# A spectral layer and an ELU block on one core: the second projection's weights and its stationary tiles at other SBUF addresses

## The chip, the cores and the metric

The kernel runs on one core of a Trainium2 chip. The metric is device time in microseconds (us). The profiled execution took 911.36 us; three timed runs have a median of 912.44 us (912.34 to 914.53).

## The reference, cut to what matters

`x` is 8 batches of 3008 tokens by 256 channels. A spectral layer comes first, then a two-layer block with an ELU:

```python
X = np.fft.rfft(x, axis=1)                       # per batch, along the tokens
Yr = Xr @ w_r - Xi @ w_i + b_r                   # complex 256 x 256 product
Yi = Xr @ w_i + Xi @ w_r + b_i
Y  = shrink(Yr) + 1j * shrink(Yi)                # toward zero by 0.01
y  = np.fft.irfft(Y, n=3008, axis=1)             # back to 24064 x 256 in all
h  = y @ w_in                                    # 256 -> 2048
g  = np.where(h > 0, h, np.exp(np.minimum(h, 0)) - 1)
out = g @ w_out                                  # 2048 -> 256
```

## The kernel before, in words

**The two halves.** The Fourier transforms are done as small matrix products with tables that the kernel builds for itself at the start. They are cut into units, named A, X, M, B and Y, whose matmuls stand at L144, L175, L192, L244 and L282. Between units the data goes to device memory and comes back in another layout (stores `DA<-A`, `DB<-Bz`, loads `Z<-DA`, `Bs<-DB`). The first batch's units run alone. Those of each later batch are laid out by `plan` between the steps of the block on the batch before, one unit per step or none.

**A step of the block.** The loop at the end of the kernel makes 376 steps: 47 blocks of 512 tokens times 8 *pairs* `fp` of hidden tiles (a tile is 128 of the 2048 hidden features, so a pair is 256). Step `i` does this:

- `front` (L705) fills a PSUM tile `hps` with four matmuls in bf16 of 512 columns (L715; a few are cut in two at a batch's end) and ScalarE takes the exponential into `Et` (L724, L726, L727 or L729).
- `finish_elu` (L734) has VectorE write the ELU of the step before into an SBUF tile `gT` (L740 or L742), 1024 elements of float32 per partition, and with that frees the step's `hps`. Two `hps` buffers take turns, and a third is used in some steps.
- `back` (L757) runs for the step two earlier (`LAG = 2`). Its eight matmuls (L773) have a 128 by 128 piece of `gT` as their stationary operand and one of the sixteen 1 KB pieces of `w_out_r` as their moving operand of 256 columns, both in the 4-byte type float32r. They add into two PSUM tiles `ps_o`, which after eight pairs are copied out (L784) and stored.

All engines' instructions run in the order in which they are written; the Tile layer adds the waits.

**The tiles of the change.** `w_out_r` is one tile of 16 pieces of 1 KB per partition, back to back. It is loaded in two halves by POOL's DMA queue (`load_w_out`, L583): the first half before the first batch's X units, the second (needed from `fp` = 4) after a small `gate` copy on POOL that waits for a load of `Bs`. `gT` comes from a pool of three buffers of 4096 bytes. The same three buffers hold, once, near the start, two tiles `A` of the second batch (L133): ScalarE and VectorE fill them and the SP queue stores them to `DA` (L157), from where `Z` of that batch is loaded (L164).

In the built kernel, `w_out_r` starts at byte 41,792 of every partition and the three `gT` buffers at 210,048, 214,144 and 218,240. The two `A` tiles take the first and the third of these. The pool gives the steps 0 and 1 the second buffer, both of them, step 2 the first and step 3 the third; from there on the three take turns.

Of the kernel before, what the change touches and what calls it, by code (L numbers as in the profile page):

```python
# [10 lines left out]
BF16 = mybir.dt.bfloat16  # L11
F32 = mybir.dt.float32
F32R = mybir.dt.float32r
# [16 lines left out]
def kernel(  # L30
# [11 lines left out]
    nc = tc.nc  # L42
    P = nc.NUM_PARTITIONS

    B, S, D = x.shape
    assert D == 256 and S == N1 * N2
    DFF = moe_w_in.shape[1]
    E = moe_w_out.shape[1]
    assert E == 256 and DFF % (2 * P) == 0
    NFT = DFF // P  # L50
# [5 lines left out]
    constp = ctx.enter_context(tc.tile_pool(name="constp", bufs=1))  # L56
# [4 lines left out]
    wcat_r = constp.tile([P, 2, 2 * D], BF16, name="wcat_r")  # L61
    wcat_s = constp.tile([P, 2, 2 * D], BF16, name="wcat_s")
    w_in_s = constp.tile([P, 2, DFF], BF16, name="w_in_s")
    w_out_r = constp.tile([P, NFT, E], F32R, name="w_out_r")
    bias_bc = constp.tile([P, 2 * D], F32, name="bias_bc")
    bias_p = constp.tile([P, 2 * D], BF16, name="bias_p")
    lam_n = constp.tile([P, 1], F32, name="lam_n")
# [22 lines left out]
    TB = 512  # L90
# [4 lines left out]
    n = B * PER  # L95
# [3 lines left out]
    A_of = {}  # L99
# [18 lines left out]
    def unit_ps(name, alone):  # L118
        if alone:
            return pre2.tile([P, 2, 512], F32, name=name, tag="pre2")  # L120
        return psF.tile([P, 2, 512], F32, name=name, tag="fps")

    def evac(dst, src, on_dve):
        if on_dve:
            nc.vector.tensor_copy(dst, src)  # L125
        else:
            nc.scalar.copy(dst, src)  # L127

    def unit_A(b, u, alone=False, on_dve=False, ahead=False):
        ci, uu = u // 2, u % 2  # L130
        if uu == 0:
            if ahead and ci > 0:
                A_of[b, ci] = late3.tile([P, 8, D], BF16, name="A", tag="gT")  # L133
            elif alone:
                A_of[b, ci] = wk4.tile([P, 8, D], BF16, name="A", tag="Bs")
            else:
                A_of[b, ci] = wk2.tile([P, 8, D], BF16, name="A", tag="A")
            if ci == 0:
                DA_of[b] = dram.tile([NJ, P, D], BF16, name="DA", tag="DA")
        xt, A = xts[ci], A_of[b, ci]  # L140
        dav = DA_of[b].rearrange("j p d -> p j d")
        ps = unit_ps("aps", alone or ahead)
        for j in range(2):
            nc.tensor.matmul(  # L144
                ps[:, j, :], lhsT=M1[:],
                rhs=xt[:, 4 * uu + 2 * j : 4 * uu + 2 * j + 2, :], start=True, stop=True,
            )
        evac(
            A[:, 4 * uu : 4 * uu + 4, :].rearrange("p n d -> p (n d)"),
            ps[:].rearrange("p a b -> p (a b)"), on_dve,  # L150
        )
        j0 = 8 * ci
        if alone:
            j0 += 4 * uu
            nc.sync.dma_start(dav[:, j0 : j0 + 4, :], A[:, 4 * uu : 4 * uu + 4, :])
        elif uu == 1:
            nc.sync.dma_start(dav[:, j0 : j0 + 8, :], A[:])  # L157
# [155 lines left out]
    with tc.tile_pool(name="stagep", bufs=1) as stagep:  # L313
# [186 lines left out]
        def fA(u):  # L500
            unit_A(0, u, alone=True)
            if u < 5:
                idle_pe(3)
# [60 lines left out]
    gatep = ctx.enter_context(tc.tile_pool(name="gatep", bufs=2))  # L564
    late2 = ctx.enter_context(tc.tile_pool(name="late2", bufs=2))
    late3 = ctx.enter_context(tc.tile_pool(name="late3", bufs=3))

    w_in_v = moe_w_in.rearrange("(c p) f -> p c f", p=P)
    w_out_v = moe_w_out.rearrange("(t p) e -> p t e", p=P).bitcast(F32R)
# [10 lines left out]

    def load_w_out(hh):
        hf = slice(hh * NFT // 2, (hh + 1) * NFT // 2)
        nc.gpsimd.dma_start(w_out_r[:, hf, :], w_out_v[:, hf, :])  # L583

    def gate(src):

# [9 lines left out]
    for ci in range(3):  # L596
        load_x(1, ci)
    load_w_out(0)
    nc.vector.tensor_scalar(w3[:], v3[:], CMAGIC, -CMAGIC, ALU.add, ALU.add)
    nc.vector.tensor_tensor(w3[:], v3[:], w3[:], ALU.subtract)  # L600
# [62 lines left out]
    for u in range(6):  # L663
        unit_A(1, u, on_dve=bool(u % 2), ahead=True)
        if u == 1:
            scale_w_in(1, True)
            for w in (2, 3):
                load_Bs(0, w)
            gate(Bs_of[0, 2][:, 0, 0:1])
            load_w_out(1)  # L670
            load_w_in(3)
        idle_pe(2)
# [22 lines left out]
    def pieces(t, k):  # L695

        out_, c = [], 0
        while c < k:
            b, r = divmod(t + c, S)
            e = min(k, c + S - r)  # L700
            out_.append((b, r, c, e))
            c = e
        return out_
# [29 lines left out]

    def finish_elu():  # L734
        for i, hps, Et, whole, halves in late_elu:
            gT = late3.tile([P, 2, TB], F32R, name="gT", tag="gT")
            for s in range(2) if halves else (slice(0, 2),):
                o, h, e = gT[:, s], hps[:, s], Et[:, s]
                if whole:
                    nc.vector.scalar_tensor_tensor(o, e, -1.0, h, ALU.add, ALU.max)  # L740
                else:
                    nc.vector.scalar_tensor_tensor(o, h, 0.0, e, ALU.max, ALU.add)  # L742
            g_of[i] = gT
        late_elu.clear()
# [12 lines left out]
    def back(i, split):  # L757
        blk, fp = divmod(i, NPAIR)
        bs = blk * TB
        gT = g_of.pop(i)  # L760
        nq = TB // P // 2
        if fp == 0:
            po_of[blk] = [
                psO.tile([P, 2, E], F32, name="ps_o", tag="outp") for _ in range(nq)
            ]
        po = po_of[blk]
        order = [(q, s) for q in range(nq) for s in range(2)]
        if i == n - 1:
            order = [(q, s) for s in range(2) for q in range(nq)]
        for q, s in order:  # L770
            ft = 2 * fp + s
            for i_ in range(2 * q, 2 * q + 2):
                nc.tensor.matmul(  # L773
                    po[q][:, i_ % 2, :], lhsT=gT[:, s, i_ * P : i_ * P + P],
                    rhs=w_out_r[:, ft, :], start=(ft == 0 and i_ % 2 == 0),
                    stop=(ft == NFT - 1), skip_group_check=True,
                )
        if fp < NPAIR - 1:
            return
        osb = late2.tile([P, 4, E], F32, name="osb", tag="osb")  # L780
        last = i == n - 1
        for q in range(nq):
            copy = nc.vector.tensor_copy if (last and q) or (split and q == 0) else nc.scalar.copy
            copy(osb[:, 2 * q : 2 * q + 2, :], po[q][:])  # L784
            for i_ in range(2 * q, 2 * q + 2):
                for b, t, c0, c1 in pieces(bs + i_ * P, P):
                    ov = out[b * S : b * S + S, :].rearrange("(r w j) e -> w r j e", w=4, j=8)
                    while c0 < c1:
                        w, r0 = t // WT, t % WT // 8
                        k = min(c1 - c0, (w + 1) * WT - t)  # L790
                        (nc.scalar if last and i_ % 2 == 0 else nc.sync).dma_start(
                            ov[w, r0 : r0 + k // 8], osb[c0 : c0 + k, i_, :]
                        )
                        t, c0 = t + k, c0 + k
        del po_of[blk]

    def put(kind, b, *a):
        return ({"A": unit_A, "X": unit_X, "M": unit_M, "B": unit_B, "Y": unit_Y}[kind], (b, *a))
# [45 lines left out]
    for i in range(n + LAG):  # L844
        if i < n:
            r = i % PER
            if r == 0:
                f0, f1 = plan(i // PER)
                used = [bool(u0 or u1) for u0, u1 in zip(f0, f1)]
            free = not used[r]  # L850
            bare = bare + 1 if free else 0
            calm = free and (i >= n - 2 or (r + 2 < PER and not used[r + 1] and not used[r + 2]))
            for f, a in f0[r]:
                f(*a)
            on_act = any(f is unit_M for f, a in f0[r])
            h = front(i, calm and bare % 3 == 1, on_act, free and i > 0)
        finish_elu()
        if i < n:
            for f, a in f1[r]:
                f(*a)  # L860
            split = i > LAG and (i - LAG) % NPAIR == NPAIR - 1
            if split:
                back(i - LAG, True)
            elu(i, *h, free and i > 0, on_act)
        else:
            split = False
        if i >= LAG and not split:
            back(i - LAG, False)
# [30 lines left out]
```

## Time and profile before

| what | us |
|---|---|
| profiled execution | 911.36 |
| its span, from first to last instruction | 909.6 |
| median of three timed runs | 912.44 |
| PE (TensorE matmuls) busy | 893.2, 98% of the span |
| VectorE busy | 717.5, 79% |
| ScalarE busy | 696.8, 77% |
| POOL busy | 314.9, 35% |
| granted TensorE clock, mean | 0.997 |

The profile has one row for each group of equal instructions: line, engine, operation, the tile written and those read, shapes, count, then the time in which at least one of them ran, the mean duration of one in ns, and the idle time in front of them with what ended it. PE is the row of the matmuls, PEld that of the loads of stationary operands (LDWEIGHTS), which run beside matmuls. Since matmuls overlap, the mean duration of one is longer than the time from one start to the next; where this document speaks of the *spacing*, it is the time between the starts of two neighbours, read from the single records of the trace.

### The profile page before, as it was taken

What the parts mean: (1) busy time and instruction counts of PE and PEld (TensorE: products, weight loads), DVE (VectorE), ACT (ScalarE), POOL (GpSimd) and SP (SyncE); (2) the same over time, 40 slices, a digit from 0 to 9 for tenths busy, and PEclk for the clock granted to TensorE, in tenths of its full rate; (3) what the DMA queues carried; (4) which work ended last, traced back from release to release, by engine and by line L of the source; (5) the groups of instructions that cost most, each with busy time, mean ns of one, the idle gap of its engine ahead of it and who ended that gap; (6) DMA issues with size and microseconds to landing.
All of it is one profiled execution on the core that took longest, in us unless ns stands there. A gap on an engine that the chain in (4) does not pass through costs nothing.

```text
span 909.6 us, 17270 instructions
## 1 busy us (share of the span) xinstructions
PE 893.2 (98%) x6721; PEld 652.3 (72%) x6721; DVE 717.5 (79%) x891; ACT 696.8 (77%) x850; POOL 314.9 (35%) x438
## 2 busy tenths in 40 slices
PE   8989999999999999999999999999999999999997
PEld 3447667876688667886678766787667866777775
DVE  8669778887788778897788877888778877778776
ACT  6768788777878778787787888778887877767664
POOL 6701540333321441405404153033332134443664
PEclk9999999999999999999999999999999999999999
DMA  8997116721283215732166032752228111231011
GB/s 270 309 269 228 47 48 186 209 70 47 77 241 124 71 47 143 190 109 85 56 201 194 24 99 59 217 161 72 69 72 230 30 42 47 82 82 48 24 48 46
DMA packets 90670, 106.24 MB, mean 117 GB/s; under 512 B 5270, under 2 KB 81308, under 8 KB 87228
## 3 DMA queue, kind: packets, MB, share of 16 engines
q1 hardware_dynamic: 84332, 77.62, 30.6%
q0 software_dynamic: 5968, 27.26, 9.1%
q8 instruction: 52, 0.85, 0.4%
q10 hardware_dynamic: 288, 0.26, 0.1%
q14 instruction: 30, 0.25, 0.1%
HBM read 55.32 MB, written 49.81 MB: 116 GB/s over the span
## 4 chain that ended last, share of the span: by engine, by line
PE 85%; DVE 5%; ACT 3%; DMA 3%; issue 2%; POOL 1%; SPq 1%; DVEq 0%; ACTq 0%; POOLq 0%
PE ps_o L773 34%; PE hps L715 34%; PE mps L192 9%; PE yps L282 2%; PE bps L244 2%; PE xps L175 2%; PE aps L144 2%; DMA Bs<-DB 2%; DVE gT L742 1%; DVE Et L754 1%; ACT Et L729 1%; ACT Et L726 1%; DMA xt<-in_x_dram 1%; DVE osb L784 1%; ACT Bz L257 1%
## 5 line engine op out<-in xcount | busy, mean ns | idle before, releaser
L773 PE MATMUL ps_o<-w_out_r,gT 128*128 128x256 f32 x3008 | 477.0, 301 | 0.2 <-DVE gT L740 0.2
L773 PEld LDWEIGHTS ps_o<-w_out_r,gT 128*128 128x128 f32 x3008 | 403.4, 189 | 50.3 <-DVE osb L784 1.3
L715 PE MATMUL hps<-yT,w_in_s 128*128 128x512 bf16 (+4 forms) x1728 | 389.9, 353 | 2.5 <-DVE gT L742 1.2
L740 DVE SCALAR_TENSOR_TENSOR gT<-Et,hps 128x512 fp32r<-128x512 f32 (+1 forms) x272 | 222.8, 848 | 75.3 <-POOL Et L752 38.2
L742 DVE SCALAR_TENSOR_TENSOR gT<-hps,Et 128x1024 fp32r<-128x1024 f32 x198 | 242.2, 1223 | 16.5 <-PE ps_o L773 1.0
L715 PEld LDWEIGHTS <-w_in_s 128*128 128x128 bf16 x1728 | 141.6, 98 | 129.4 <-issue 23.0
L729 ACT ACTIVATE Et<-hps 128x1024 f32<-128x1024 f32 x198 | 204.0, 1030 | 13.2 <-PE hps L715 6.7
L752 POOL TENSOR_SCALAR Et<-Et 128x512 f32<-128x512 f32 x187 | 111.4, 615 | 222.9 <-ACT Et L724 222.9
L754 DVE TENSOR_SCALAR Et<-Et 128x1024 f32<-128x1024 f32 x198 | 137.0, 692 | 48.0 <-ACT Et L729 40.1
L210 POOL TENSOR_SCALAR clip<-yb 128x512 f32<-128x512 f32 x84 | 51.7, 615 | 316.0 <-DVE yb L202 278.6
L724 ACT ACTIVATE Et<-hps 128x512 f32<-128x512 f32 x188 | 102.1, 595 | 63.9 <-PE hps L715 63.9
L726 ACT ACTIVATE Et<-hps 128x1024 f32<-128x1024 f32 x84 | 86.3, 1027 | 71.5 <-PE hps L715 71.0
L211 POOL TENSOR_TENSOR Y<-yb,clip 128x512 bf16<-128x512 f32 x84 | 107.2, 1276 | 7.0
L727 ACT ACTIVATE Et<-Et 128x1024 f32<-128x1024 f32 x84 | 88.8, 1058 | 2.7
L202 DVE TENSOR_TENSOR yb<-mps,bias_bc 128x512 f32<-128x512 f32 x89 | 61.4, 689 | 35.4 <-PE mps L192 28.6
L127 ACT CAST XT<-xps 128x768 bf16<-128x768 f32 x61 | 48.8, 800 | 15.8 <-PE xps L175 15.8
L127 ACT CAST yT<-yps 128x752 bf16<-128x752 f32 x63 | 49.7, 788 | 14.2 <-PE yps L282 14.1
L192 PE MATMUL mps<-wcat_r,XT 128*128 128x512 bf16 x192 | 58.2, 384 | 0.8 <-ACT Bz L257 0.3
L127 ACT CAST A<-aps 128x1024 bf16<-128x1024 f32 x45 | 45.6, 1014 | 15.3 <-PE aps L144 13.8
L192 PE MATMUL mps<-wcat_s,XT 128*128 128x512 bf16 x192 | 57.1, 379 | 0.0
L192 PEld LDWEIGHTS <-XT 128*128 128x128 bf16 x384 | 30.8, 98 | 29.6 <-DVE XT L125 0.6
L257 ACT CAST Bz<-bps 128x1024 bf16<-128x1024 f32 x46 | 46.0, 1000 | 2.5 <-PE bps L244 2.5
(110 smaller groups left out, 412.9 us busy)
## 6 DMA issues: line engine op xcount, KB each, us to landing
xt<-in_x_dram POOLq DMA_DIRECT2D x21, 1024.0 KB, 7.1
out_dram<-osb SPq DMA_DIRECT2D x158, 128.0 KB
Bs<-DB SPq DMA_DIRECT2D x32, 384.0 KB
DA<-A SPq DMA_DIRECT2D x21, 512.0 KB
DB<-Bz SPq DMA_DIRECT2D x21, 512.0 KB
Z<-DA SPq DMA_DIRECT2D x7, 1152.0 KB
Z<-DA SPq DMA_DIRECT2D x11, 384.0 KB
xt<-in_x_dram POOLq DMA_DIRECT2D x6, 512.0 KB, 5.9
```

Of the source, the lines that this page charges most:

```text
L127: nc.scalar.copy(dst, src)
L192: nc.tensor.matmul(ps, lhsT=XT[:, dt, c, o : o + P], rhs=wm[:, dt, :], start=(not biased and m == 0 and dt == 0), stop=(m == 1 and dt == 1),)
L211: nc.gpsimd.tensor_tensor(Y_of[b, q][:, i, :], yb, clip[:], ALU.subtract)
L715: nc.tensor.matmul(hps[:, s, c0:c1], lhsT=w_in_s[:, dt, ft * P : ft * P + P], rhs=yT_of[b][:, dt, t0 : t0 + c1 - c0], start=(dt == 0), sto ...
L724: nc.scalar.activation(E_[:, s], hps[:, s], AF.Exp)
L726: nc.scalar.activation(E_, hps[:], AF.Relu, scale=-1.0)
L729: nc.scalar.activation(E_, hps[:], AF.Exp)
L740: nc.vector.scalar_tensor_tensor(o, e, -1.0, h, ALU.add, ALU.max)
L742: nc.vector.scalar_tensor_tensor(o, h, 0.0, e, ALU.max, ALU.add)
L752: eng.tensor_scalar(E_[:, s], E_[:, s], 1.0, 0.0, ALU.min, ALU.max)
L754: nc.vector.tensor_scalar(E_, E_, 1.0, -1.0, ALU.min, ALU.add)
L773: nc.tensor.matmul(po[q][:, i_ % 2, :], lhsT=gT[:, s, i_ * P : i_ * P + P], rhs=w_out_r[:, ft, :], start=(ft == 0 and i_ % 2 == 0), stop=( ...
```

## The change

Three things are edited.

- `w_out_r` becomes eight rows of 2080 bytes, one per pair: two pieces of 1 KB back to back and then 32 bytes that nothing uses. Pair `fp` thus lies 32 times `fp` bytes further than before. The tile is 256 bytes longer.
- Each half of it is loaded by two DMAs of 4 pieces a partition in place of one of 8.
- The `gT` buffers become three tiles of their own, 4608 bytes each, used from byte 0, 16 and 256 on. Step `i` uses number `(i + 2) mod 3`; the two early `A` tiles use number 0 and 1.

```diff
-    w_out_r = constp.tile([P, NFT, E], F32R, name="w_out_r")
+    w_out_r = constp.tile([P, NFT // 2, 2 * E + 8], F32R, name="w_out_r")
...
-                A_of[b, ci] = late3.tile([P, 8, D], BF16, name="A", tag="gT")
+                A_of[b, ci] = shifted(ci - 1, 8 * D, BF16, "A").rearrange("p (n d) -> p n d", d=D)
...
+    late1 = ctx.enter_context(tc.tile_pool(name="late1", bufs=1))
+    SHIFT = (0, 16, 256)
+
+    def shifted(k, n_, dt, name):
+
+        k %= 3
+        o = SHIFT[k] * n_ // (8 * TB)
+        w_ = n_ + 512 * n_ // (8 * TB)
+        t = late1.tile([P, w_], dt, name=name, tag=f"gT{k}")
+        return t[:, o : o + n_]
...
-        nc.gpsimd.dma_start(w_out_r[:, hf, :], w_out_v[:, hf, :])
+        pairs = slice(hh * NFT // 4, (hh + 1) * NFT // 4)
+        for t in range(2):
+            nc.gpsimd.dma_start(
+                w_out_r[:, pairs, t * E : t * E + E],
+                w_out_v[:, hf, :].rearrange("p (a t) e -> p a t e", t=2)[:, :, t, :],
+            )
...
-            gT = late3.tile([P, 2, TB], F32R, name="gT", tag="gT")
+            gT = shifted(i + 2, 2 * TB, F32R, "gT").rearrange("p (s t) -> p s t", s=2)
...
-                    rhs=w_out_r[:, ft, :], start=(ft == 0 and i_ % 2 == 0),
+                    rhs=w_out_r[:, fp, s * E : s * E + E], start=(ft == 0 and i_ % 2 == 0),
```

In the built kernel after the change every tile that lies behind `w_out_r` has moved by 256 bytes, and the `gT` data of the three buffers start at 210,304, 214,928 and 219,776. The order of the instructions on every engine is the same as before, but for the two added DMAs on POOL's queue; some waits differ, as other DMAs and other users of a buffer have to be waited for.

## The prediction

> **What bounds the kernel.** I read the engine totals first, then the chain of work that ended last, then the groups by shape, and at last the timeline of one ordinary step.
>
> ```profile
> PE 893.2 (98%) x6721; PEld 652.3 (72%) x6721; DVE 717.5 (79%) x891; ACT 696.8 (77%) x850; POOL 314.9 (35%) x438
> PE 85%; DVE 5%; ACT 3%; DMA 3%; issue 2%; POOL 1%; SPq 1%; DVEq 0%; ACTq 0%; POOLq 0%
> ```
>
> PE is busy 98% of the span and carries 85% of the chain. Whatever changes the spacing of its matmuls changes the time one for one; whatever slows another engine costs nothing until PE waits for it.
>
> ```profile
> L773 PE MATMUL ps_o<-w_out_r,gT 128*128 128x256 f32 x3008 | 477.0, 301 | 0.2 <-DVE gT L740 0.2
> L773 PEld LDWEIGHTS ps_o<-w_out_r,gT 128*128 128x128 f32 x3008 | 403.4, 189 | 50.3 <-DVE osb L784 1.3 <-DVE gT L742 0.5 <-DVE gT L740 0.4
> L715 PEld LDWEIGHTS <-w_in_s 128*128 128x128 bf16 x1728 | 141.6, 98 | 129.4 <-issue 23.0 <-DVE gT L740 0.5 <-DVE gT L742 0.4
> ```
>
> The change moves the two operands of the first row and of nothing else that is large. A stationary load in 4-byte data takes 189 ns, in bf16 98 ns. One ordinary step, timeline with start and duration in us:
>
> ```profile
> 500.00 0.57 PEld L715 LDWEIGHTS <-w_in_s 128*128 128x128 bf16 x4
> 500.70 1.10 PEld L773 LDWEIGHTS ps_o<-w_out_r,gT 128*128 128x128 f32 x8
> 501.83 0.37 PEld L175 LDWEIGHTS <-Z 96*128 96x128 bf16 x8
> ```
>
> From the first load of `back` (500.70) to the first load of the next unit (501.83) are 1.13 us, in which the last bf16 matmul still streams for 0.22 us. The eight matmuls thus need 0.91 us, 114 ns each. The trace's single records say the same: of 2,244 spacings within the eights (the first, which holds that bf16 matmul, the last and seven long ones left out) 914 are 113 to 115 ns, 1,237 are 117 or more, and the mean is 116.1. Matmuls of the same 256 columns in bf16 (the cut pieces of L715) stand 109 ns apart. So the load of the next 4-byte stationary piece, not the stream, sets the pace, and the stream has 4 to 9 ns to spare.
>
> **What the addresses do now.** In the kernel before, all starts of `w_out_r`'s pieces are equal modulo 512 bytes, and so are those of `gT`'s pieces. No record can thus show what the offsets of 16 to 256 bytes do. What can be read is larger offsets: sixteen pieces of `w_out_r`, three `gT` buffers. The median of the sum of five inner spacings is 573 ns in every one of the three buffers, and 572 to 574 ns for seven of the eight pairs (582 for pair 0, whose steps follow the copies of `ps_o`). The two spacings, 113 and 118, follow the place of the step within a batch, batch after batch, while buffer and pair at that place change. They hang on what runs beside the step, not on addresses this far apart.
>
> **The change part by part.**
>
> *Operand offsets.* 3,008 matmuls are touched. One end: every spacing comes down to the short one, 113.3 ns. That is 2.8 ns on 7 spacings of 376 steps, 2.8 x 2,632 = 7.4 us less. If even the load were hidden, down to 109 ns, it would be 7.1 x 2,632 = 18.7 us less. Other end: a load that does not start on some wider boundary reads one stretch more. From the two load rows, 91 ns for 256 more bytes a partition, a byte costs 0.36 ns; 32 bytes too many cost 11 ns, 64 cost 23. One buffer of three is 16 bytes off, 1,003 loads: 11 to 23 us more. The streams of the four odd pairs, 32 bytes off, can take 64 bytes more in 1024, 6% of 107 ns or about 7 ns, and have 4 to 9 to spare. I take 0, by the nearest row: that of the offsets that do vary. A second reason: a 512-byte load and a 1024-byte stream both walk through all starts modulo 512, so an offset changes when two reads meet in the same place, not whether they do.
>
> [...]
>
> *Who holds which buffer at the start.* This is a definite cost. Before, steps 0 and 1 share one buffer, so the second ELU waits for the matmuls that read the first:
>
> ```profile
> 61.93 1.28 PE L773 MATMUL ps_o<-w_out_r,gT 128*128 128x256 f32 x8
> 63.25 1.23 DVE L742 SCALAR_TENSOR_TENSOR gT<-hps,Et 128x1024 fp32r<-128x1024 f32 x1 [1.04 <-PE ps_o L773]
> 64.53 1.02 PE L715 MATMUL hps<-yT,w_in_s 128*128 128x512 bf16 x4 [0.96 <-DVE gT L742]
> 65.11 1.22 DVE L742 SCALAR_TENSOR_TENSOR gT<-hps,Et 128x1024 fp32r<-128x1024 f32 x1
> 66.67 1.03 PE L715 MATMUL hps<-yT,w_in_s 128*128 128x512 bf16 x4
> 66.83 0.82 SPq L164 DMA_DIRECT2D Z<-DA  x2
> ```
>
> After, step 0 has a buffer of its own and that wait goes, but step 1 takes the buffer of the first early `A` and step 2 that of the second, one step sooner than before (then: steps 2 and 3). They wait for the stores of these `A`. The trace's semaphore records have the last parts of the two stores land at 64.10 and 66.64 us; the `Z` load at 66.83, which needs both, agrees. So the ELU of step 1 starts at 64.14 in place of 63.25. That of step 2 starts at 66.66 in place of 65.11, 1.55 us late. Behind it on VectorE stand a scaling of `w_in_s` (0.42) and the first operation and ELU of step 3 (0.69 + 1.23), and PE's `front` of steps 3, 4 and 5 waits for these ELUs to free `hps`: +0.9, +1.3, +1.4 us. VectorE then gains some 0.2 us a step (0.69 + 1.23 against a step of 2.15), but what PE has lost by then stays lost: it has no idle time later to absorb it. I take 1.5 us, bounds 0.8 and 2.2, since the stores' landings can move by some 0.7 us as the split load of `w_out_r` runs in the same time.
>
> *The split loads.* POOL's two issues take 1.12 and 0.97 us; two more cost at most the same again. At the first, POOL next sits idle for 3.16 us before its first `clip`, which hides it; without that cover it would be 1.1 us in the start. The second half is issued at 59.87, lands at 69.45 and is first read at 71.65, 73.1 after the delay above; 1 us later still lands in time. Bytes and piece size are the same. POOL is then idle until 75.43. Nothing.
>
> *VectorE's writes, and all other tiles moved by 256 bytes.* Nothing: VectorE is 79% busy, and every tile keeps its place modulo 256.
>
> *Sum.* 911.36 of the profiled execution + 1.5 + 0 = 912.9. The median of the runs lies 1.08 above that execution; against it the forecast is 912.44 + 1.5 = **913.9 us**.
>
> **Rivals.**
>
> *Offsets help (chance 0.27).* If the 118 ns spacing comes from loads that meet the stream or VectorE's writes, spreading 24 combinations of buffer and pair thins it out. From 4.2 us less (a smaller gain counts with no effect) to the 7.4 of the short spacing, against 913.9: 906.5 to 909.7; at the floor of 109 ns 895. For it: two sharp values of spacing. Against it: both occur with the same offsets.
>
> *Offsets hurt (chance 0.30), ending slower.* The mechanism is the load of buffer 1, 16 bytes off, reading 32 or 64 bytes more: 913.9 + 11 to 23 = 925 to 937; if only a part shows because the load has slack behind it, from 916 on. It decides from 1.3 ns per matmul of that buffer, as loads set the pace. For it: no operand of PE starts off a multiple of 32 bytes now. Against it: no row has such a start, so nothing bears it out.
>
> *The start goes worse (0.05).* If the second half of `w_out_r` or the stores land 2 us later than taken, 915.5 to 918.
>
> *The change does not do what it says.* The buffers lie 256, 784 and 1536 bytes from their old places, not 0, 16 and 256, but modulo 256 the shifts are 0, 16 and 0, so it comes close; it is in the cases above.
>
> **How the numbers follow.** No effect of the offsets has 0.38, 913.2 to 914.7. 0.3% is 2.7 us, about what a measurement of this kernel can tell from no change: this case is within it. Faster 0.27, within 0.38, slower 0.35. The range leaves out about a tenth at either side: the deep gain towards 895, and the full 64-byte cost. It is 905 to 925.
>
> **What would show it.** In the profile after: L773 with 477 us and load spacings of 113 and 118 as before, equal for the three buffers; the second and third L742 at 64.1 and 66.7 us, their idle time ended by DMA; PE's L715 at 67.9 where it was 66.67. A third of the steps with longer spacings would prove the misaligned load. Fewer spacings of 118 would prove the gain. If both are absent and the time still moves by more than 3 us, my account of what sets the pace is wrong.

## The result and the profile after

The changed kernel takes 919.57 us (median of four runs, 918.11 to 921.96) against 912.39 us for the kernel before in the same runs. The ratio is 1.0077, with a 95% interval of 1.0057 to 1.0097: slower by 7.2 us. The forecast was 913.9, in a range of 905 to 925; slower by over 0.3% had a chance of 0.35.

The profiled execution took 919.79 us with a span of 918.0, against 911.36 and 909.6: 8.4 us more. Engine totals, chain of work by engine, and the two rows of the moved operands, from the page of the kernel after (L773 is now L788):

```profile
PE 892.5 (97%) x6617; PEld 656.3 (71%) x6721; DVE 718.0 (78%) x891; ACT 697.5 (76%) x850; POOL 315.8 (34%) x440
...
PE 87%; DMA 4%; ACT 3%; DVE 2%; issue 2%; POOL 1%; SPq 1%; ACTq 0%; DVEq 0%; POOLq 0%
...
L788 PE MATMUL ps_o<-w_out_r,gT 128*128 128x256 f32 x3008 | 483.8, 303 | 0.1
L788 PEld LDWEIGHTS ps_o<-w_out_r,gT 128*128 128x128 f32 x3008 | 408.2, 189 | 50.2 <-DVE osb L799 0.7
```

The matmuls on `w_out_r` and `gT` are busy for 483.8 us where it was 477.0. (Records of 104 other matmuls are missing from this trace, so PE's own total cannot be compared; all 3,008 of this row are there.) The mean of one load of `gT` is still 189 ns: what has grown is the time between them. The single records give a spacing of 118.3 ns, against 116.1. (The first spacing of each eight is left out, as it holds a bf16 matmul, and so are the last step and spacings of 150 ns and more.)

The second place is the start. The timeline of the kernel after, steps 0 to 4 (start, duration in us, and in brackets the idle time before it and what ended it):

```profile
61.85 1.27 PE L788 MATMUL ps_o<-w_out_r,gT 128*128 128x256 f32 x8
...
64.72 1.22 DVE L757 SCALAR_TENSOR_TENSOR gT<-hps,Et 128x1024 fp32r<-128x1024 f32 x1 [3.00 <-DMA DA<-A]
...
66.00 1.87 PE L730 MATMUL hps<-yT,w_in_s 128*128 128x512 bf16 x4 [2.52 <-DVE gT L757]
...
67.30 2.19 PE L788 MATMUL ps_o<-w_out_r,gT 128*128 128x256 f32 x8
...
68.96 1.22 DVE L757 SCALAR_TENSOR_TENSOR gT<-hps,Et 128x1024 fp32r<-128x1024 f32 x1 [2.42 <-DMA DA<-A]
...
70.24 1.02 PE L730 MATMUL hps<-yT,w_in_s 128*128 128x512 bf16 x3 [0.40 <-DVE gT L757]
```

The second and third ELU now wait for the stores of the early `A` tiles, and PE's `front` waits for them. The chain of work shows the same as one piece, the last store, from its issue to its landing:

```profile
56.23 12.61 DMA DA<-A
```

There is a third thing in these rows. Four bf16 matmuls take 1.87 us where four took 1.02, and eight on `w_out_r` take 2.19. Here is the same stretch of both kernels, before first (its length, the busy time and count of PE, PEld, VectorE, ScalarE and POOL, then granted clock, DMA share and GB/s):

```profile
66.00:69.50 3.50, 3.50 (x37) 2.68 (x36) 3.41 (x6) 2.91 (x4) 0.00 (x0) 1.00 1.13 293
```

```profile
62.00:66.00 4.00, 1.48 (x18) 1.31 (x18) 1.28 (x2) 1.81 (x2) 0.03 (x1) 0.98 1.21 333
66.00:69.50 3.50, 3.50 (x16) 2.53 (x16) 1.08 (x2) 1.03 (x1) 0.00 (x0) 0.53 0.94 234
```

In the kernel after PE worked for 1.48 us of the 4.00 us before 66.00, and then its clock was granted at 0.53 of full speed over 3.5 us. The clock records give 3,413 ns at one half, from 65.85 on; PE had then been idle for 2.37 us, since 63.47. No run shows what sets the slow clock off.

The slow clock did not make the kernel slower here. Behind it PE waits again, for 0.40 us at 70.24, for the third ELU, and that ELU waits for a store; at the full clock PE would have waited longer. Nor is a slow stretch new. The kernel before has one of the same 3,413 ns, from 57.45 on, ahead of step 0's `back`:

```profile
58.00:62.00 4.00, 3.76 (x26) 2.18 (x24) 2.40 (x3) 3.24 (x4) 1.47 (x2) 0.64 1.03 284
```

From the start of step 0's `back` to that of step 8 are 22.3 us after and 18.3 before, 4.0 more. From step 8 to the start of the last of these matmuls the trace has 828.5 us after and 824.0 before, 4.5 more. So the loss has two parts. The first is the late ELU: counted from step 0's `back`, the third ELU starts at 7.11 us after and at 3.18 before, 3.9 later.

### The profile page after: what moved, and what is told of

Read it like the earlier page. It is cut to its first block, busy times and chain, and to the rows that moved or that the text cites. A ratio compares the mean times of both kernels' runs of the same rounds, so it can differ in the third digit from the quotient of the medians.

```text
span 918.0 us, 17168 instructions
## 1 busy us (share of the span) xinstructions
PE 892.5 (97%) x6617; PEld 656.3 (71%) x6721; DVE 718.0 (78%) x891; ACT 697.5 (76%) x850; POOL 315.8 (34%) x440
## 4 chain that ended last, share of the span: by engine, by line
PE 87%; DMA 4%; ACT 3%; DVE 2%; issue 2%; POOL 1%; SPq 1%; ACTq 0%; DVEq 0%; POOLq 0%
PE ps_o L788 36%; PE hps L730 34%; PE mps L192 9%; PE xps L175 2%; PE yps L282 2%; PE bps L244 2%; PE aps L144 2%; DMA Bs<-DB 2%; DMA DA<-A 1%; ACT Et L741 1%; DMA xt<-in_x_dram 1%; ACT Bz L257 1%; SPq L806 0%; DVE gT L755 0%; DMA DB<-Bz 0%
## 5 line engine op out<-in xcount | busy, mean ns | idle before, releaser
L788 PE MATMUL ps_o<-w_out_r,gT 128*128 128x256 f32 x3008 | 483.8, 303 | 0.1
L788 PEld LDWEIGHTS ps_o<-w_out_r,gT 128*128 128x128 f32 x3008 | 408.2, 189 | 50.2 <-DVE osb L799 0.7
L730 PE MATMUL hps<-yT,w_in_s 128*128 128x512 bf16 (+7 forms) x1650 | 383.1, 352 | 9.0 <-DVE gT L757 3.8
L192 PE MATMUL mps<-wcat_r,XT 128*128 128x512 bf16 x180 | 55.6, 384 | 0.8 <-ACT Bz L257 0.3
L192 PE MATMUL mps<-wcat_s,XT 128*128 128x512 bf16 x182 | 54.9, 379 | 0.7
```

Source lines behind the costliest of these rows:

```text
L192: nc.tensor.matmul(ps, lhsT=XT[:, dt, c, o : o + P], rhs=wm[:, dt, :], start=(not biased and m == 0 and dt == 0), stop=(m == 1 and dt == 1),)
L730: nc.tensor.matmul(hps[:, s, c0:c1], lhsT=w_in_s[:, dt, ft * P : ft * P + P], rhs=yT_of[b][:, dt, t0 : t0 + c1 - c0], start=(dt == 0), sto ...
L788: nc.tensor.matmul(po[q][:, i_ % 2, :], lhsT=gT[:, s, i_ * P : i_ * P + P], rhs=w_out_r[:, fp, s * E : s * E + E], start=(ft == 0 and i_ % ...
```

## The experiments

Theory 1 says that there are two causes: the new owners of the buffers cost time at the start, and the offsets lengthen the spacing. The rival says that there is one: the late start puts the steps into a worse rhythm for the rest. The table has all runs; every ratio is to the kernel before, measured together with the run. (Its medians were 912.39 beside the kernel after, 912.11 beside own_tiles to gt_offsets, 913.04 beside both_16 to gt_32_48_64 and four_gt, and 911.92 beside the rest.) "Start" is the time from step 0 to step 8 in the profiled execution, "rest" from there to the start of the last matmul on `w_out_r`, both in us; "spacing" is in ns.

| kernel | median us | ratio, 95% interval | spacing | start | rest |
|---|---|---|---|---|---|
| before | 912.39 | | 116.1 | 18.3 | 824.0 |
| after | 919.57 | 1.0077, 1.0057 to 1.0097 | 118.3 | 22.3 | 828.5 |
| own_tiles | 914.77 | 1.0032, 1.0018 to 1.0045 | 116.2 | 21.2 | 823.7 |
| after_old_owners | 917.05 | 1.0053, 1.0041 to 1.0065 | 118.4 | 19.0 | 828.5 |
| wout_rows | 917.07 | 1.0053, 1.0041 to 1.0065 | 118.1 | 20.1 | 827.8 |
| gt_offsets | 914.80 | 1.0032, 1.0020 to 1.0044 | 117.3 | 19.0 | 825.8 |
| both_16 | 913.61 | 1.0004, 0.9993 to 1.0014 | 116.7 | 18.8 | 824.2 |
| rows_64 | 915.50 | 1.0024, 1.0013 to 1.0036 | 117.6 | 19.1 | 827.3 |
| gt_32_48_64 | 918.14 | 1.0055, 1.0035 to 1.0074 | 118.6 | 18.5 | 829.2 |
| gt_512 | 912.23 | 1.0004, 0.9995 to 1.0013 | 116.4 | 18.7 | 824.0 |
| both_512 | 911.91 | 1.0006, 0.9996 to 1.0015 | 116.2 | 18.5 | 823.3 |
| w_128_gt_256 | 914.11 | 1.0022, 1.0013 to 1.0032 | 117.0 | 18.9 | 824.9 |
| four_gt | 911.86 | 0.9989, 0.9979 to 0.9999 | 116.1 | 17.5 | 824.3 |
| four_gt_128 | 913.38 | 1.0017, 1.0008 to 1.0026 | 116.9 | 17.7 | 825.6 |

"Start" is one execution each. Among the ten kernels with the old owners it goes from 18.3 to 20.1, by when the second early store lands: at 66.64 us before, too early for any ELU to wait, at 69.28 in wout_rows, where the fourth ELU starts at 69.40.

### One cause or two

**own_tiles**: the new owners alone, every address as before.

```diff
+    SHIFT = (0, 0, 0)
...
+        w_ = n_ + 0 * n_ // (8 * TB)
...
-            gT = late3.tile([P, 2, TB], F32R, name="gT", tag="gT")
+            gT = shifted(i + 2, 2 * TB, F32R, "gT").rearrange("p (s t) -> p s t", s=2)
```

> The kernel before, with the three gT buffers as tiles of their own at their old addresses and in the order of the change (step 1 takes the buffer of the first early A, step 2 that of the second); no offset, w_out_r as before. Theory 1 (two causes: the start loses time by the buffers' owners, the offsets lengthen the spacing of the matmuls): the start is 2 to 4 us late by step 8, the spacing stays at 116.1 ns, the time is 914.5 to 916.5. Rival (one cause: the late start puts the steps into a worse rhythm for good): 917 to 920, spacing 118.

Measured: spacing 116.2, 2.7 us slower. Its timeline at the same place:

```profile
64.96 1.23 DVE L752 SCALAR_TENSOR_TENSOR gT<-hps,Et 128x1024 fp32r<-128x1024 f32 x1 [2.70 <-DMA DA<-A]
...
66.23 1.74 PE L725 MATMUL hps<-yT,w_in_s 128*128 128x512 bf16 x4 [2.20 <-DVE gT L752]
...
68.39 1.22 DVE L752 SCALAR_TENSOR_TENSOR gT<-hps,Et 128x1024 fp32r<-128x1024 f32 x1 [1.61 <-DMA DA<-A]
```

The waits for the stores and the slow matmuls after them (1.74 us for four) are here without any offset, and without a split load of `w_out_r`. Counted from step 0's `back`, the third ELU is 2.8 us later than before, and the start 2.9 us longer. The rest of the kernel runs as before (823.7 us against 824.0): the late start did not change the rhythm. The rival falls.

**after_old_owners**: all offsets of the change, the old owners.

```diff
-            gT = shifted(i + 2, 2 * TB, F32R, "gT").rearrange("p (s t) -> p s t", s=2)
+            gT = shifted(max(i, 1) + 1, 2 * TB, F32R, "gT").rearrange("p (s t) -> p s t", s=2)
```

> The kernel after, but steps 0 and 1 share one buffer again and steps 2 and 3 take those of the early A, as before the change; all offsets kept. Theory 1: the loss at the start goes, the spacing stays at 118.3 ns, the time is 916 to 917.5. One-cause rival: 912.5, spacing 116.1.

Measured: 917.05, spacing 118.4, start 19.0. The loss against the kernel before falls from 7.2 to 4.9 us: some 2.3 us were the start, and what remains comes with the spacing, but for the 0.7 us that the start of this execution is longer. Both halves of theory 1 hold.

### Which operand

**wout_rows** is the kernel before with the edits of the change to `w_out_r` and its load alone. All that lies behind `w_out_r`, `gT` too, thus lies 256 bytes further, as after the change.

> The kernel before, with w_out_r alone in rows of 2080 bytes and loaded by two DMAs a half; gT from the old pool. Theory 1: no loss at the start, spacing between 116.1 and 118.3 ns; if the rows alone make the longer spacing 917, if the gT offsets do 912.5. One-cause rival: 912.5, spacing 116.1.

**gt_offsets** is the kernel before with `SHIFT = (0, 16, 256)` and the old owners alone.

> The kernel before, with gT at offsets 0, 16 and 256 alone, in the old order of owners; w_out_r as before. Theory 1: no loss at the start; if a stationary load 16 bytes off is what costs, the buffer at 16 alone has a longer spacing, and the time is 913 to 915; if the rows of w_out_r are what costs, 912.5. One-cause rival: 912.5.

Either alone lengthens the spacing, to 118.1 and to 117.3, and costs 5.0 and 2.7 us by the medians. In the rest, where the start plays no part, they cost 3.8 and 1.8 us, and together (after_old_owners) 4.5: less than the sum. In gt_offsets the three buffers can be told apart in one timeline, as every third step has the buffer at 16. Loads of `gT` of three whole steps in a row:

```profile
251.94 1.10 PEld L783 LDWEIGHTS ps_o<-w_out_r,gT 128*128 128x128 f32 x8
...
254.20 1.10 PEld L783 LDWEIGHTS ps_o<-w_out_r,gT 128*128 128x128 f32 x8
...
256.46 1.12 PEld L783 LDWEIGHTS ps_o<-w_out_r,gT 128*128 128x128 f32 x8
```

Eight loads take 1.12 us from the buffer at 16 and 1.10 from the others. Over the whole kernel the spacing is 116.2 ns for the buffer at 0, 118.8 for that at 16 and 116.9 for that at 256. The buffer at 0 is as fast as before, next to slow ones.

### A start off a boundary, or the distance between the operands

**both_16**: every piece of both operands 16 bytes further.

```diff
-    w_out_r = constp.tile([P, NFT, E], F32R, name="w_out_r")
+    w_out_t = constp.tile([P, NFT * E + 128], F32R, name="w_out_r")
+    w_out_r = w_out_t[:, 4 : 4 + NFT * E].rearrange("p (t e) -> p t e", e=E)
...
+    SHIFT = (16, 16, 16)
```

> The kernel before, with every piece of w_out_r and every gT buffer 16 bytes further, so that the two keep their distance modulo 512; old owners. If the cost lies in where each operand starts by itself (theory A: a start off some boundary wider than 16 bytes costs): spacing 118.8 ns or more in all three buffers, 919 to 920 (2.6 ns x 2,632 = 6.9 us). If it lies in the distance between the two operands (theory B: the two reads of the matmul meet): spacing 116.1, 912 to 913.5.

**gt_32_48_64**: `SHIFT = (32, 48, 64)`, old owners.

> The kernel before, with the gT buffers at offsets 32, 48 and 64, w_out_r as before, old owners. Theory A with a boundary of 64: the buffer at 64 at 116.1, those at 32 and 48 at 118 to 119, 915.5. With a boundary of 32: those at 32 and 64 at 116.1, that at 48 at 118.8, 914. Theory B: three different values, that at 64 not at 116.1.

Both speak against theory A. With 16 bytes on both sides the spacing is 116.7, only 0.6 above that of before (theory B expected none), though every load and every stream starts 16 bytes off; the time is that of before. With `gT` alone at 64, a multiple of 64, it is 118.9, no better than at 48 (118.7) and worse than at 32 (118.0). So it isn't the place of the load by itself: moving `gT` against `w_out_r` cost up to 2.8 ns here, moving both together 0.6.

**rows_64**: rows of 2112 bytes in place of 2080 (`2 * E + 16`).

> The kernel before, with w_out_r in rows of 2112 bytes, 64 apart in place of 32, everything behind it moved by 512; gT from the old pool. Theory A with a boundary of 64: spacing 116.1 in all eight pairs, 912 to 913.5. Theory A with a wider boundary or theory B: pair 0 at 116.3, as its distance is that of before, pairs 1 to 7 at 117 to 119, 915 to 917.

Theory A with a boundary of 64 falls here too: the time is 915.5. But theory B's number for pair 0 fails as well, 118.0 where 116.3 was expected (117.6 without five spacings of over 130 ns). Pairs 1 to 7 have 118.6, 115.8, 118.9, 117.3, 118.5, 115.5 and 118.6: pairs 2 and 6, 128 and 384 bytes off, are the quickest, at or below the quickest pairs of the kernel before (115.8).

### How far the distance alone explains it

**gt_512** puts 512 unused bytes behind `w_out_r`, **both_512** puts them in front of its data (`w_out_t[:, 128 : ...]`), **w_128_gt_256** gives the data 128 and all that lies behind it 256 bytes.

> The kernel before with 512 unused bytes behind w_out_r, so that gT and all other later tiles lie 512 bytes further; nothing else. If only the distance modulo 512 counts: spacing 116.1 ns in all pairs, 912 to 913.5. If the distance counts modulo 1024 (the length of a moving piece; pair 0 of the kernel with rows of 2112 bytes had this distance and 118.0 ns): 118.0 in all pairs, 916 to 918.

> The kernel before with 512 unused bytes in front of w_out_r's data, so that w_out_r, gT and all tiles between lie 512 bytes further and keep their distance. Distance theory: 116.1 ns, 912 to 913.5. If the place of each operand counts: another spacing than 116.1.

> The kernel before with w_out_r's data 128 bytes further and gT 256 bytes further, uniformly in all pairs. The distance is 128 larger than before. If the distance alone counts, modulo 1024: 115.5 ns, as pair 6 of the rows of 2112 bytes had with this distance, 911 to 912.5. If not the distance alone: 117.4 ns, as pair 4 of the rows of 2080 bytes had with these very addresses modulo 1024, 915 to 917.

gt_512 has 116.4 and both_512 116.2, both in the time of before: 512 bytes made no difference above 0.3 ns, in distance or place. The 118.0 of pair 0 in rows_64, where gt_512 has 116.7 for that pair at just the same addresses, is thus not a matter of its own two operands alone: what the other pairs do seems to change it. w_128_gt_256 has 117.0, neither of the two values expected, and 116.6 to 117.3 in every pair. A distance tried in one pair among others does not show what it is worth in all of them.

### Four buffers

**four_gt**: four buffers at addresses that agree modulo 512 with the old ones, and owners chosen so that no ELU at the start waits.

```diff
+    SHIFT = (0, 0, 0, 0)
...
-            gT = late3.tile([P, 2, TB], F32R, name="gT", tag="gT")
+            gT = shifted(2 + i % 2 if i < 4 else i, 2 * TB, F32R, "gT").rearrange("p (s t) -> p s t", s=2)
```

> The kernel before with four gT buffers at addresses that agree modulo 512 with the old ones; steps 0 to 3 use the two that no early A has held, step 4 and 5 then those two. No ELU at the start waits for matmuls or for a store. If the start's loss is those waits: 0.9 us at step 1 and up to 2 us at step 3 go, the second to fourth ELU start by about 62.3, 64.3 and 66.4 us, the spacing is 116.1, 910 to 911.5. If another wait takes their place: 912.

The ELUs of steps 1 and 2 in its timeline, and the `front` after each:

```profile
63.63 1.22 DVE L752 SCALAR_TENSOR_TENSOR gT<-hps,Et 128x1024 fp32r<-128x1024 f32 x1
...
65.09 1.03 PE L725 MATMUL hps<-yT,w_in_s 128*128 128x512 bf16 x4
...
65.94 1.22 DVE L752 SCALAR_TENSOR_TENSOR gT<-hps,Et 128x1024 fp32r<-128x1024 f32 x1
...
67.25 1.03 PE L725 MATMUL hps<-yT,w_in_s 128*128 128x512 bf16 x3
```

No bracket is left. In this execution step 0 itself came 1.7 us later than in that of before, so the absolute times are later than expected; from step 0 to step 8 it needs 17.5 us where before needs 18.3. The start is shorter than in all ten kernels with the old owners (18.3 to 20.1). The ratio of 0.9989 has its interval only just below 1: about 1.0 us faster than the kernel before, if at all, and 7.7 faster than the one after, by their medians (911.86 and 919.57, not taken side by side).

**four_gt_128** adds the distance of the quick pair 2 of rows_64 to it, in all pairs (`w_out_t[:, 32 : ...]` of a tile 512 bytes longer).

> The kernel with four gT buffers, with w_out_r's data 128 and gT 512 bytes further, the distance that pair 2 of the rows of 2112 bytes had (115.8 ns; pair 6, with another one, 115.5). If what was seen in single pairs holds for a whole kernel: spacing 115.5 to 115.8, and 1 us less than the four-buffer kernel, 910 to 911.5. If the spacing hangs on the steps around as well: 116 to 118, 912 to 916.

A miss: 116.9 ns and slower than before. Its start is as short as that of four_gt (17.7), and the spacing takes it back. The old distance, modulo 512, is the best of those tried for the whole kernel.

## Why the prediction came out as it did

**What bounds the kernel: right as to PE, open as to the load.** PE sets the time. 2.2 ns more on some 2,632 spacings are 5.8 us; the trace has 4.5 from step 8 on, and the runs 4.9 in after_old_owners. From step 8 on the spacings within the eights add up to 5.2 us more (369.1 against 363.9), and the time from one eight to the next is 0.7 shorter (458.3 against 459.0). That the load of `gT`, not the stream, sets the spacing was argued from the 109 ns of bf16, and no run tells the two apart. The prediction had named a sign that its account of the pace is wrong: neither a third of the steps slower nor fewer spacings of 118, and yet a change of over 3 us. Both were absent, and the spacing alone brought 4.5 us, so by that sign the account of the pace does not hold.

**"I take 0" for the operand offsets: this step failed.** The measured term is 4.5 to 4.9 us. The row it went by had offsets of 1,024 bytes and more, all equal modulo 512. gt_512 and both_512 agree with that row: 512 bytes more gave 116.4 and 116.2 ns. It said nothing about 16 to 256 bytes, and 0 was taken for them all the same. The second reason, that both reads walk through all starts modulo 512 so that an offset changes only when they meet, fell with gt_offsets: 16 bytes alone were worth 2.6 ns (118.8 against 116.2), while 16 bytes on both operands (both_16) gave 116.7.

**The rival "offsets hurt": right in its sign, wrong in its mechanism and price.** It had a load off a boundary read 32 or 64 bytes more, 11 to 23 ns a load. both_16 and gt_32_48_64 rule the boundary out, and the buffer at 16 lost 2.6 ns. The test that I had named for it, a third of the steps with longer spacings, did not come out either: in the kernel after all three buffers are slow (117.9, 118.7 and 118.2).

**The owners of the buffers: right mechanism, too small.** The waits came where they were forecast, at the second and third ELU, ended by the stores. Forecast were 64.14 and 66.66 us; it was 64.72 and 68.96, as the stores landed at 64.60 and 68.84 in place of 64.10 and 66.64. I took 1.5 us with a bound of 2.2; own_tiles makes it 2.7, the pair after and after_old_owners 2.3. The landing in the profiled execution of before was an early one: in the other 13 traces the second store lands between 66.82 and 70.42. One execution was not enough for a bound of 0.7. With a landing that late the old owners wait as well, at the fourth ELU: it starts 0.12 us behind the landing in eight of their ten traces. The new owners wait for the same store one step sooner, so by estimate they lose about one step, 2.3 us (the third and fourth ELU of the kernel after start at 68.96 and 71.22).

**The split loads: not waited for, the rest open.** The second half of `w_out_r` landed at 67.9 and 69.25, in time. By the medians own_tiles, without a split, loses as much at the start. But the second store takes 11.35 to 12.61 us from issue to landing in the four kernels with split loads (12.2 on average) and 10.29 to 12.00 in the ten without (11.3), so a delay by the split is neither shown nor excluded.

**The sum.** 2.7 for the start and 4.9 for the spacing are 7.6; measured were 7.2. The forecast of 913.9 was 5.7 us too low, most of it the offsets' term. That the range, 905 to 925, holds the measured time owes much to luck: its upper part stood for loads of `gT` 11 to 23 ns longer, and the loads of the kernel after take 189 ns on average, as those of the kernel before.

**What stays open.** Why the distance counts is not shown: that two reads collide in the memory is an argument, no more. Nor is it shown why a pair's spacing seems to depend on the offsets of other pairs (pair 2 has 115.8 in rows_64 and 116.7 in four_gt_128, with the same two addresses modulo 512). VectorE's writes into `gT` were always moved with `gT`; a part of theirs in it has not been tried apart.

## What to carry to other kernels

When a trace shows no difference between places, look at what those places have in common before you infer that place does not matter: here all were equal modulo 512, and the offsets of the change were smaller. Before buffers get owners of their own, list for the first few rounds who held each buffer and when its last reader, a store included, is done; a pool's odd choice of buffers can be the better one. A landing time from one profiled execution is one draw; a wait that is to hang on it needs a bound from several.

## What the runs showed of the hardware

The relative place of the moving and the stationary operand of float32r matmuls of 256 columns changed their spacing by up to 2.8 ns in 116 (gt_32_48_64, buffer at 64), and 16 bytes were enough for 2.6 (gt_offsets, buffer at 16), while 512 bytes (gt_512, 116.4) and common shifts of 16 and 512 bytes (both_16, 116.7; both_512, 116.2) changed it by 0.6 ns at most. In the kernel after, 2.37 us into a stall of PE of 2.52 us, 3,413 ns at half the clock began: four matmuls took 1.87 us instead of 1.02, and the next eight 2.19 instead of 1.27. This fell into a wait and cost nothing. One and the same store of 512 KB, the second early `A`, landed 10.3 to 12.6 us after its issue in the 14 traces.
